# A fused forward and backward kernel on one core: plain loads in place of transposing and scattered ones at the start, and another order of the first transposes

## The chip, the cores and the metric

The kernel runs on one core of a Trainium2 chip. The metric is the device time of one execution in microseconds; the time before is the median of three runs. A second source is the profile of one further execution, with a record of every instruction on every engine and of every transfer. All positions in time below ("at 21.0 us") are counted from the start of that profiled execution.

## What is computed

The reference runs a block forward and then differentiates it with respect to all inputs but `B_x`; the kernel writes the output and eight gradients.

```python
mod = (silu(c) @ w_mod).reshape(1, 6, 1, -1)        # c: 1 x 576, w_mod: 576 x 3456
sa, ca, ga, sb, cb, gb = (mod[:, i] for i in range(6))
h = layernorm(x) * (1 + ca) + sa                    # x: 1 x 2048 x 576, bf16
x = x + ga * irfft2(rfft2(h) * (w_r + 1j * w_i))
h = layernorm(x) * (1 + cb) + sb
x = x + gb * (((h @ w_gate) * (h @ w_up)) @ w_down) # w_down: 4608 x 576
# outputs: x, and the vector-Jacobian product for grad_out (2048 x 576)
```

Three things of this matter for the change. The gate `gb` is one of the six modulation rows, so it needs `silu(c)` and a sixth of `w_mod`. The gradient that flows back into the hidden layer is `(gb * grad_out) @ w_down^T`; it needs `grad_out` turned so that the model dimension lies on the partitions, scaled by `gb`, and `w_down` turned likewise. And `x` is normalised and modulated before the Fourier transform.

## The kernel before

All of SBUF is one tile, `arena`, cut by byte offsets into views; PSUM is one tile, `bank`, of eight banks. Work is written out by hand for TensorE (PE): its instructions run in the order of the program. The order of VectorE (DVE), ScalarE (ACT), GpSimd (POOL) and SyncE (SP) is set by a scheduler, and each of them then runs its list strictly in that order. SP issues nearly all loads, POOL issues the stores of `ghh_d`.

The start of the kernel (lines 207 to 245) issues the first loads on SP in this order: `c` spread over 96 partitions (L209), a sixth of `w_mod` called `wm_a` (L212), `grad_out` in four groups `go` (L217), the first two of eighteen blocks of `w_down` by a transposing DMA (`load_wdT`, L232 and L233, two DMAs a block), `x` in four groups `xs` (L237), two more pieces of `w_mod` (`wm_b`, `wm_c`, L212 again), and the Fourier tables `TB`, `TC`, `TI`, `TBI` (L241 to L245). ACT issues `BD`, which holds the identity for transposes (L215). POOL issues four further small loads of `c` in other column layouts (L222 to L224).

PE then computes `gb` as a column (L257: 30 matmuls of one column each), turns `grad_out` into `goT` (`go_transposes`, L301: 80 transposes; ACT at L304 and DVE at L306 copy each group of four out of PSUM, 512 wide, times the `gb` column), and comes to the normalisation.

A queue called `fill` holds PE work that may go anywhere: 18 blocks of `w_down` by two couples, each couple four pieces (L324, L328, L331, L332), each block giving 256 rows of the hidden gradient; ACT copies them out (L336) and POOL stores them (L337). Block p needs its turned `w_down` block; the piece that starts block p asks for block p + 2 (`f0`, L340). `fill.run(us)` takes pieces off the queue until their nominal cost reaches the credit given. So the credits, not the clock, decide how much of this work lies between other stages.

Then, for each of four groups `jg` of `x`: `norm1(jg + 1)` (row statistics on DVE at L367 and L368, an inverse square root by small DVE operations L374 to L381, and the rows on ACT at L553), modulation and folding on DVE (L567, L568, L387, L388), `fill.run(7.5)`, the first Fourier stage `stage_a` on PE (L394, L397, L398) with its copy on ACT (L404, L412), and one pair of modulation rows (`mod_rows`, L272, copied out at L275 by ACT and L277 or L279 by DVE). PSUM banks 0 to 2 go round between the transposes, `stage_a` and `mod_rows` through `single()`.

Later stages: eight units of the middle Fourier stages, then a loop of 17 steps for the inverse transform and the second layer norm (L524 to L538 on PE, L532, L533, L685 to L687, L703, L704 on DVE, 2.7 us of `fill` each step), a flush of what is left in `fill`, and the block over the hidden layer (L745 to L756), whose right-hand side `h2T` comes by four transposing DMAs (`ln2_turn`, L690). From there on nothing is touched by the change.

Of the kernel before, what the change touches and what calls it, by code (L numbers as in the profile page):

```python
# [81 lines left out]
def build(ctx, tc, A_x, A_w_r, A_w_i, B_w_gate, B_w_up, B_w_down, c_in, w_mod, grad_out,  # L82
# [52 lines left out]
    def span(base, n, size):  # L135
        return [base + i * size for i in range(n)]
# [61 lines left out]
    wm_a, wm_b, wm_c = V(ST, [6, D]), V(ST + 71168, [6, 2 * D]), V(ST + 6912, [6, 3 * D])  # L198
    wm_t = {SGB: wm_a, SSA: wm_b[:, :, 0:D], SCA: wm_b[:, :, D:], SGA: wm_c[:, :, 0:D], SSB: wm_c[:, :, D:2 * D], SCB: wm_c[:, :, 2 * D:]}
    sc_rep = V(ST + 27648, [6, 128])  # L200
    h1_r = Ring([ACC + 24832, ACC + 29440], [4, D])
    st_r = Ring([ACC + 24224, ACC + 24416], [4, 2, 6], FP32)
    mv_r = Ring([ACC + 24608, ACC + 24640], [4, 2], FP32)
# [1 line left out]

    with tc.manual_schedule(engines={PE}):

        with nc.allow_non_contiguous_dma(reason="tiny c load"):
            sp.dma_start(c_bf[0:96, :], c_in[0, :].rearrange("(m q) -> q m", q=96))  # L209

        def load_wm(eng, t, s0, s1):
            eng.dma_start(t[0:96], w_mod[:, s0 * D:s1 * D].rearrange("(m q) n -> q m n", q=96))  # L212

        load_wm(sp, wm_a, 5, 6)
        ac.dma_start(BD.rearrange("p a b -> p (a b)"), tabs["BD"][:, :])  # L215
        for jg in range(4):
            sp.dma_start(go[:, 4 * jg:4 * jg + 4, :], go_v[:, 4 * jg:4 * jg + 4, :])  # L217
        ve.memset(ones[:], 1.0)
        po.memset(c2_bf[:], 0.0)
        with nc.allow_non_contiguous_dma(reason="tiny c loads"):  # L220
            for h in range(2):
                po.dma_start(c2_bf[64 * h:64 * h + 64, 0:9], c_in[0, :].rearrange("(m q) -> q m", q=64))  # L222
            po.dma_start(c2_bf[:, 9:13], c_in[0, 0:512].rearrange("(m q) -> q m", q=128))
            po.dma_start(c2_bf[0:64, 13:14], c_in[0, 512:576].rearrange("(m q) -> q m", q=64))  # L224

        wdt = {}

        def load_wdT(p):
            t = WdT_r.next()
            wdt[p] = t  # L230
            rows = B_w_down[256 * p:256 * p + 256, :]
            sp.dma_start_transpose(out=t[:, 0:4, :], in_=rows[:, 0:512])  # L232
            sp.dma_start_transpose(out=t[:, 4, :], in_=rows[:, 448:576])  # L233

        load_wdT(0)
        for jg in range(4):
            sp.dma_start(xs[:, 4 * jg:4 * jg + 4, :], x_v[:, 4 * jg:4 * jg + 4, :])  # L237
            if jg == 0:
                load_wm(sp, wm_b, 0, 2)
        load_wdT(1)  # L240
        sp.dma_start(TB.rearrange("p a b -> p (a b)"), tabs["TB"][:, :])  # L241
        load_wm(sp, wm_c, 2, 5)
        sp.dma_start(TC.rearrange("p a b c -> p (a b c)"), tabs["TC"][:, :])
        sp.dma_start(TI.rearrange("p a b c -> p (a b c)"), tabs["TI"][:, :])
        sp.dma_start(TBI.rearrange("p a b -> p (a b)"), tabs["TBI"][:, :])  # L245


        q96 = slice(0, 96)
        ve.tensor_copy(c_f[q96], c_bf[q96])
        act(sig[q96], c_f[q96], ACT.Sigmoid)  # L250
        tt(sc_bf[q96], c_f[q96], sig[q96], MUL)
        for m in range(6):
            ve.tensor_copy(sc_rep[q96, m, :], sc_bf[q96, m:m + 1].to_broadcast([96, 128]))
        for dk in range(5):
            d0 = 448 if dk == 4 else 128 * dk
            for m in range(6):
                mm(bank[:, 0, dk:dk + 1], wm_a[0:96, m, d0:d0 + 128], sc_bf[0:96, m:m + 1], m == 0, m == 5)  # L257
        ve.tensor_copy(gb_bf[:], bank[:, 0, 0:5])
        ve.tensor_copy(gbcol[:], gb_bf[:])

        sbank = [0]

        def single():
            sbank[0] = (sbank[0] + 1) % 3
            return sbank[0]
# [14 lines left out]

        def silu_columns():

            c2, s2 = small[:, 82:96], small[:, 50:64]
            c2_bf_all = c2_bf[:, :]
            ve.tensor_copy(c2, c2_bf_all)
            act(s2, c2, ACT.Sigmoid)
            tt(c2_bf_all, c2, s2, MUL)
            ve.tensor_copy(sc64, c2_bf[:, 0:9])
            t = dsl5
            ts(t, s2[:, 9:14], -1.0, 1.0, MUL, ADD)  # L290
            tt(t, t, c2[:, 9:14], MUL)
            ts(t, t, 1.0, None, ADD)
            tt(t, t, s2[:, 9:14], MUL)

        def go_transposes(jg):
            for m in range(5):
                b = single()
                pt = bank[:, b, 0:256].bitcast(BF)
                d0 = 448 if m == 4 else 128 * m
                for jj in range(4):  # L300
                    pe.transpose(pt[:, 128 * jj:128 * jj + 128], go[:, 4 * jg + jj, d0:d0 + 128], ident)  # L301
                dst = goT[:, m, 512 * jg:512 * jg + 512]
                if m % 2 == 0 or jg == 0:
                    act(dst, pt, ACT.Copy, scale=gbcol[:, m:m + 1])  # L304
                else:
                    ts(dst, pt, gbcol[:, m:m + 1], None, MUL)  # L306


        dpair = [0]
# [7 lines left out]
        def ghh_couple(p, sb):  # L317

            b0 = [0, 0]
            cs = [slice(512 * (sb + i), 512 * (sb + i) + 512) for i in range(2)]  # L320

            def full_a(i):
                for k, m in enumerate(range(4)):
                    mm(bank[:, b0[i], :], wdt[p][:, m, 0:128], goT[:, m, cs[i]], i == 0 and k == 0, i == 1 and k == 3)  # L324

            def full_b(i):
                for k, m in enumerate((0, 1, 2, 4)):
                    mm(bank[:, b0[i] + 1, :], wdt[p][:, m, 128:256], goT[:, m, cs[i]], i == 0 and k == 0, i == 1 and k == 3)  # L328

            def rem(i):  # L330
                mm(bank[:, b0[i], :], wdt[p][64:128, 4, 0:128], goT[64:128, 4, cs[i]], i == 1, i == 0)  # L331
                mm(bank[:, b0[i] + 1, :], wdt[p][0:64, 3, 128:256], goT[0:64, 3, cs[i]], i == 1, i == 0)  # L332

            def evac(i):
                st = ghst_r.next()
                ac.copy(st[:], bank[:, b0[i]:b0[i] + 2, :])  # L336
                po.dma_start(ghh_d[p, :, :, cs[i]], st[:])  # L337

            def f0():
                if sb == 0 and p + 2 < NP:  # L340
                    load_wdT(p + 2)
                b0[0] = dbank()
                b0[1] = dbank()
                full_a(0)

            def f1():
                full_b(0)
                rem(0)
                evac(0)
                rem(1)  # L350

            def f3():
                full_b(1)
                evac(1)
            fill.add(0.87, f0)
            fill.add(1.4, f1)
            fill.add(0.87, lambda: full_a(1))
            fill.add(0.87, f3)

        for p in range(NP):  # L360
            for sb in (0, 2):
                ghh_couple(p, sb)


        def row_stats(src, st, mv, jj):
# [42 lines left out]
        def evac_rem(eng, brem, j0, n):  # L408
            dst = At[0:64, 4, :, 8 * j0:8 * (j0 + n)].rearrange("p c (j b) -> p j c b", j=n)
            src = bank[0:64, brem, 0:128 * n].rearrange("p (j c b) -> p j c b", j=n, c=16)  # L410
            if eng is ac:
                ac.copy(dst, src)  # L412
            else:
                ve.tensor_copy(dst, src)
# [130 lines left out]
        def norm1(jg):  # L545
            j0 = 4 * jg
            st, mv = st_r.next(), mv_r.next()
            for jj in range(4):
                row_stats(xs[:, j0 + jj, :], st, mv, jj)
            inv_std(mv, rstd1, nmr1, j0)  # L550
            h1s[jg] = h1_r.next()
            for j in range(j0, j0 + 4):
                act(h1s[jg][:, j - j0, :], xs[:, j, :], ACT.Identity, bias=nmr1[:, j:j + 1], scale=rstd1[:, j:j + 1])  # L553

        norm1(0)
        for jg in range(4):
            go_transposes(jg)
        silu_columns()
        fill.run(7.0)
        mod_rows(SSA)  # L560
        mod_rows(SCA)
        for jg in range(4):
            j0 = 4 * jg
            if jg < 3:
                norm1(jg + 1)
            h1 = h1s[jg]
            tt(h1[:], h1[:], opca_b, MUL)  # L567
            tt(h1[:], h1[:], sa_b, ADD)  # L568
            fold(Ft[:, j0:j0 + 4, :], h1, 4)
            fill.run(7.5)  # L570
            for jj in range(4):
                b = single()
                stage_a(Ft[:, j0 + jj, :], b)
                evac_a(ac, b, j0 + jj)
            for jj in range(4):
                stage_a_rem(Ft[:, j0 + jj, :], 3, jj)
            evac_rem(ac, 3, j0, 4)
            mod_rows((SGA, SSB, SCB, SGB)[jg])


# [827 lines left out]
```

## Time and profile before

| | |
|---|---|
| Median of 3 runs | 1545.58 us (1545.24 to 1550.46) |
| Profiled execution: device time | 1546.08 us |
| Profiled execution: first to last instruction | 1544.3 us |
| Mean granted PE clock | 0.987 |
| PE busy | 1474.5 us, 95% |
| DVE busy | 782.4 us, 51% |
| ACT busy | 556.2 us, 36% |

A line of a profile page's part with engines gives busy time and share of the span. In a window table each line is one stretch of time: the busy time of each engine with the number of its instructions in brackets, then the granted PE clock (1.00 is full speed), the mean busy share of the 16 DMA engines, and the rate of all transfers in GB/s. In a table of waits a line reads "who (engine, tile, line) <- who released it: total us, how often, longest". In a timeline a line has a start, a duration, the engine, the line of the program and the operation.

### The profile page before, as it was taken

Reading aid. Unit: us, or ns where it says so; the run is one execution under the profiler, and the core shown is the slowest. Engines: PE = TensorE matmul, PEld = TensorE weight load, DVE = VectorE, ACT = ScalarE, POOL = GpSimd, SP = SyncE. Lnnn points to the kernel's source line nnn. Section 1 sums busy time; section 2 is a strip of 40 time slices with the busy share of each in tenths; the row PEclk is TensorE's granted clock in tenths of the full one; section 3 lists DMA queues with packets and bytes.
Section 4 is the critical chain, followed back from the end, with each engine's and each line's share of the span. In section 5 each row is a group of like instructions: output and inputs, shape, how many; then the busy total and the mean of one; then the engine's idle time right before and its main releaser. Section 6 shows DMA issues by size and latency. Waiting matters only on the chain.

```text
span 1544.3 us, 28343 instructions
## 1 busy us (share of the span) xinstructions
PE 1474.5 (95%) x11213; PEld 984.0 (64%) x11236; DVE 782.4 (51%) x1733; ACT 556.2 (36%) x1064; POOL 265.3 (17%) x389
## 2 busy tenths in 40 slices
PE   6799998999999999999999999999999988899997
PEld 3344443586686677677667668668667676676665
DVE  5523487533533533543543453353354775787555
ACT  5656676212203212212221221220321575334664
POOL 1122422122122112112202202211201101000000
PEclk9899999999999999999999999999999999999998
DMA  9765787885476467558548557657645679797752
GB/s 251 211 142 162 200 234 182 182 176 134 110 153 157 114 131 167 123 112 183 124 96 183 130 111 157 142 113 144 162 114 106 157 192 295 194 245 198 200 171 86
DMA packets 444903, 248.77 MB, mean 161 GB/s; under 512 B 323104, under 2 KB 422240, under 8 KB 444256
## 3 DMA queue, kind: packets, MB, share of 16 engines
q1 hardware_dynamic: 421376, 176.53, 51.2%
q0 software_dynamic: 22624, 69.62, 15.1%
q8 instruction: 88, 1.44, 0.4%
q10 hardware_dynamic: 768, 0.79, 0.2%
q14 instruction: 47, 0.39, 0.1%
HBM read 95.58 MB, written 74.20 MB: 110 GB/s over the span
## 4 chain that ended last, share of the span: by engine, by line
PE 72%; issue 16%; DVE 4%; DMA 3%; SPq 3%; ACT 2%; POOL 0%; POOLq 0%; DVEq 0%; ACTq 0%
PE bank L750 8%; PE bank L781 8%; PE bank L752 8%; PE bank L828 7%; PE bank L832 7%; PE bank L887 5%; PE bank L889 4%; PE bank L890 4%; PE bank L888 4%; PE bank L324 3%; PE bank L328 3%; PE bank L745 2%; PE bank L848 2%; DMA arena<-in_B_w_down_dram 1%; SPq L232 1%
## 5 line engine op out<-in xcount | busy, mean ns | idle before, releaser
L901 DVE TENSOR_TENSOR arena<-arena,bank 128x576 f32<-128x576 f32 x256 | 193.0, 754 | 305.2 <-PE bank L890 305.2
L756 ACT CAST arena<-bank 128x512 bf16<-128x512 f32 x144 | 84.4, 586 | 391.0 <-PE bank L746 373.6
L887 PE MATMUL bank<-arena 128*128 128x288 bf16 x576 | 164.3, 285 | 3.0 <-ACT arena L833 2.8
L890 PE MATMUL bank<-arena 128*128 128x288 bf16 x576 | 164.9, 286 | 0.0
L889 PE MATMUL bank<-arena 128*128 128x288 bf16 x576 | 164.7, 286 | 0.0
L888 PE MATMUL bank<-arena 128*128 128x288 bf16 x576 | 164.4, 285 | 0.0
L750 PE MATMUL bank<-arena 128*128 128x512 bf16 x576 | 149.4, 382 | 1.0 <-ACT arena L756 1.0
L828 PE MATMUL bank<-arena 128*128 128x256 bf16 x1152 | 149.7, 273 | 0.6 <-ACT arena L833 0.6
L1025 PE MATMUL bank<-arena 128*128 128x288 bf16 x1152 | 149.7, 287 | 0.0
L832 PE MATMUL bank<-arena 128*128 128x256 bf16 x1152 | 149.3, 273 | 0.0
L752 PE MATMUL bank<-arena 128*128 128x512 bf16 x576 | 148.7, 381 | 0.0
L1025 PEld LDWEIGHTS <-arena 128*128 128x128 bf16 x1152 | 111.8, 98 | 31.7 <-issue 3.3
L781 PE MATMUL bank<-arena 128*128 128x288 bf16 x1024 | 128.1, 286 | 0.0
L828 PEld LDWEIGHTS <-arena 128*128 128x128 bf16 x1152 | 110.9, 98 | 17.6 <-issue 4.6
L832 PEld LDWEIGHTS <-arena 128*128 128x128 bf16 x1152 | 112.3, 98 | 13.7 <-issue 0.4
L833 ACT CAST arena<-bank 128x256 bf16<-128x256 f32 x144 | 53.5, 372 | 185.3 <-PE bank L832 185.3
L781 PEld LDWEIGHTS <-arena 128*128 128x128 bf16 x1024 | 100.2, 98 | 28.2
L760 DVE TENSOR_TENSOR arena<-arena 128x512 bf16<-128x512 bf16 x144 | 61.2, 425 | 107.4 <-ACT arena L756 107.4
L750 PEld LDWEIGHTS <-arena 128*128 128x128 bf16 x576 | 50.4, 98 | 79.8 <-issue 31.8
L752 PEld LDWEIGHTS <-arena 128*128 128x128 bf16 x576 | 56.6, 98 | 68.6 <-issue 1.1
L757 ACT CAST arena<-bank 128x512 bf16<-128x512 f32 x144 | 84.8, 589 | 23.7 <-PE bank L752 23.7
L336 ACT CAST arena<-bank 128x1024 bf16<-128x1024 f32 x72 | 72.7, 1010 | 53.3 <-PE bank L332 25.8
(247 smaller groups left out, 2243.1 us busy)
## 6 DMA issues: line engine op xcount, KB each, us to landing
ghh_d<-arena POOLq DMA_DIRECT2D x72, 256.0 KB, 3.5
arena<-ghh_d POOLq DMA_DIRECT2D x36, 512.0 KB, 5.4
hh_d<-arena SPq DMA_DIRECT2D x36, 512.0 KB, 4.3
arena<-hh_d SPq DMA_DIRECT2D x16, 1152.0 KB, 7.2
out_dram<-arena POOLq DMA_DIRECT2D x36, 256.0 KB, 5.1
arena<-in_B_w_down_dram POOLq DMA_DIRECT2D x18, 288.0 KB, 4.1
out_dram<-arena POOLq DMA_DIRECT2D x36, 144.0 KB, 5.5
arena<-in_B_w_gate_dram POOLq DMA_DIRECT2D x18, 256.0 KB, 3.5
```

The lines of the kernel that those rows point to most:

```text
L750: mm(bank[:, bg, :], w[:, m, fs], h2T[:, js, m, :], odd == 0 and m == 0, odd == 1 and m == 3)
L752: mm(bank[:, bu, :], w[:, 4 + k, fs], h2T[:, js, m, :], odd == 0 and k == 0, odd == 1 and k == 3)
L757: ac.copy(u[:], bank[:, bu, :])
L781: mm(bank[:, b0 + h, 0:288], sf[:, 0, fb, j, :], go[:, j, 288 * h:288 * h + 288], j == 0, j == 15)
L828: mm(bank[:, st["b"], 0:256], h2p[:, j, 128 * m:128 * m + 128], sf[:, 1 + w, :, j, :], j == 0, False)
L832: mm(bank[:, st["b"], 0:256], h2p[:, j, 128 * m:128 * m + 128], sf[:, 1 + w, :, j, :], False, j == 15)
L887: mm(o, xT[:, 1, 0, cs], wT[p][:, 0, 0, hs], True, False)
L888: mm(o, xT[:, 2, 0, cs], wT[p][:, 0, 1, hs], False, False)
L889: mm(o, xT[:, 1, 1, cs], wT[p][:, 1, 0, hs], False, False)
L890: mm(o, xT[:, 2, 1, cs], wT[p][:, 1, 1, hs], False, True)
L901: tt(dst, dst, src, ADD)
L1025: mm(bank[:, yb, 0:288], hl[:, fb % 18, 128 * (j % 2):128 * (j % 2) + 128], wdr[:, fb, 288 * h:288 * h + 288], fb == 0, fb == 35)
```

## The change

The change touches only the first part of the program.

1. `c` comes as one row on one partition (`c_row`, 1,152 B). 29 matmuls of one column against a one spread it into the column layouts that were loaded before; POOL's four loads and its memset are gone.
2. Blocks 0 to 2 of `w_down` come as plain loads (`wdn`, rows of 1,152 B) into the area that `At` takes later. `turn_wd` turns each with ten PE transposes into two banks, and ACT copies them out (1024 and 256 wide). Block 0 is turned among the gradient's transposes; blocks 1 and 2 are pieces of `fill`, with a nominal cost of 1.2 us each, after the first couple of blocks 0 and 1. Blocks from 3 on come by the transposing DMA as before.
3. The order of the loads on SP is new; `go` 0 is first after `c_row`.
4. The first 20 gradient transposes stand ahead of the gate on PE. Pairs of groups share a bank, and they are copied out 1024 wide, ten copies in place of twenty.
5. The rows of `norm1` are split off (`norm1_rows`) and written after `mod_rows` or after `stage_a`, not before.

```diff
-        with nc.allow_non_contiguous_dma(reason="tiny c load"):
-            sp.dma_start(c_bf[0:96, :], c_in[0, :].rearrange("(m q) -> q m", q=96))
...
-        load_wm(sp, wm_a, 5, 6)
+        sp.dma_start(c_row[0:1, :], c_in[0:1, :])
         ac.dma_start(BD.rearrange("p a b -> p (a b)"), tabs["BD"][:, :])
...
+        def load_wdn(p):
+            sp.dma_start(wdn[p][:], B_w_down[256 * p:256 * p + 256, :].rearrange("(j f) d -> f j d", f=128))
+
+        load_go(0)
+        load_wm(wm_a, 5, 6)
+        load_go(1)
+        load_wdn(0)
+        load_go(2)
+        load_go(3)
+        load_xs(0)
+        load_wm(wm_b, 0, 2)
+        load_wdn(1)
+        load_xs(1)
+        load_xs(2)
+        load_wdn(2)
+        load_xs(3)
+        sp.dma_start(TB.rearrange("p a b -> p (a b)"), tabs["TB"][:, :])
+        load_wm(wm_c, 2, 5)
...
-        po.memset(c2_bf[:], 0.0)
-        with nc.allow_non_contiguous_dma(reason="tiny c loads"):
-            for h in range(2):
-                po.dma_start(c2_bf[64 * h:64 * h + 64, 0:9], c_in[0, :].rearrange("(m q) -> q m", q=64))
-            po.dma_start(c2_bf[:, 9:13], c_in[0, 0:512].rearrange("(m q) -> q m", q=128))
-            po.dma_start(c2_bf[0:64, 13:14], c_in[0, 512:576].rearrange("(m q) -> q m", q=64))
...
-        load_wdT(0)
-        for jg in range(4):
-            sp.dma_start(xs[:, 4 * jg:4 * jg + 4, :], x_v[:, 4 * jg:4 * jg + 4, :])
-            if jg == 0:
-                load_wm(sp, wm_b, 0, 2)
-        load_wdT(1)
...
+        def turn_wd(p, b0, b1):
+
+            t = wdt[p] = WdT_r.t[p % 3]
+            for b, m0, m1 in ((b0, 0, 4), (b1, 4, 5)):
+                pt = bank[:, b, :].bitcast(BF)
+                for m in range(m0, m1):
+                    d0 = 448 if m == 4 else 128 * m
+                    for fb in range(2):
+                        c0 = 256 * (m - m0) + 128 * fb
+                        pe.transpose(pt[:, c0:c0 + 128], wdn[p][:, fb, d0:d0 + 128], ident)
+                ac.copy(t[:, m0:m1, :].rearrange("p m f -> p (m f)"), pt[:, 0:256 * (m1 - m0)])
...
-        ve.tensor_copy(c_f[q96], c_bf[q96])
+        cp = bank[:, 5, 128:160]
+        for m in range(6):
+            mm(cp[0:96, m:m + 1], c_row[0:1, 96 * m:96 * m + 96], ones[0:1, 0:1], True, True)
+        ve.tensor_copy(c_f[q96], cp[q96, 0:6])
...
+        GB = ((0, 1, 2, 3, 4), (5, 0, 1, 2, 3))
+        for m in range(5):
+            turn_go(0, m)
         for dk in range(5):
             d0 = 448 if dk == 4 else 128 * dk
             for m in range(6):
-                mm(bank[:, 0, dk:dk + 1], wm_a[0:96, m, d0:d0 + 128], sc_bf[0:96, m:m + 1], m == 0, m == 5)
+                mm(bank[:, 5, dk:dk + 1], wm_a[0:96, m, d0:d0 + 128], sc_bf[0:96, m:m + 1], m == 0, m == 5)
...
+        for m in range(5):
+            turn_go(1, m)
+            evac_go(0, m)
+        turn_wd(0, 6, 7)
+        for jg in (2, 3):
+            for m in range(5):
+                turn_go(jg, m)
+                if jg == 3:
+                    evac_go(1, m)
...
-                if sb == 0 and p + 2 < NP:
+                if sb == 0 and 3 <= p + 2 < NP:
                     load_wdT(p + 2)
...
         for p in range(NP):
             for sb in (0, 2):
                 ghh_couple(p, sb)
+                if sb == 0 and p < 2:
+                    fill.add(1.2, lambda p=p: turn_wd(p + 1, single(), single()))
...
+        silu_columns()
         norm1(0)
-        for jg in range(4):
-            go_transposes(jg)
-        silu_columns()
         fill.run(7.0)
         mod_rows(SSA)
         mod_rows(SCA)
+        norm1_rows(0)
...
             evac_rem(ac, 3, j0, 4)
+            if jg < 3:
+                norm1_rows(jg + 1)
             mod_rows((SGA, SSB, SCB, SGB)[jg])
```

## The prediction, made before the changed kernel was run

> **What bounds the kernel now.** I read the page's slices first: PE is busy nearly all the time, except at the very start, in the second slice and once near 265 us. Only there can a change of the first loads win or lose.
>
> ```profile
> PE   6799998999999999999999999999999988899997
> PEclk9899999999999999999999999999999999999998
> ```
>
> Then the windows of the first 60 us, the waits up to 62 us, and the timeline of the same stretch.
>
> ```profile
> 0.00:10.00 10.00, 0.96 (x30) 0.88 (x30) 1.53 (x9) 1.49 (x2) 3.32 (x9) 1.00 0.75 149
> 20.00:30.00 10.00, 9.75 (x62) 4.79 (x61) 9.00 (x36) 6.13 (x9) 1.39 (x2) 1.00 1.11 256
> 40.00:50.00 10.00, 6.26 (x43) 3.65 (x43) 9.19 (x37) 8.97 (x14) 0.69 (x1) 0.83 1.01 400
> 50.00:60.00 10.00, 6.02 (x20) 1.97 (x21) 5.78 (x16) 4.54 (x7) 1.23 (x2) 0.66 0.84 166
> ...
> PE bank L257 <- DMA arena<-in_w_mod_dram: 7.6, 1, 7.6
> PE bank L324 <- DMA arena<-in_B_w_down_dram: 4.7, 1, 4.7
> PE bank L394 <- ACT arena L404: 2.9, 1, 2.9
> PE bank L272 <- ACT arena L275: 1.4, 1, 1.4
> ```
>
> PE does 1 us of work in the first ten. The transfer engines are mostly full from 4 us to 58 us, yet move only 149 to 400 GB/s. Where PE waits at 40 to 58 us the granted clock falls to about half, so the matmuls after the wait cost double. The longest wait is for block 2 of `w_down`: its transposing loads occupy SP and land at 53.9 us.
>
> ```profile
> 4.18 6.66 SPq L232
> 15.84 9.61 SPq L232
> ...
> 31.31 22.62 DMA arena<-in_B_w_down_dram
> 53.94 0.04 issue
> 53.98 1.89 PE bank L324 x4
> ```
>
> Last, the windows around the end of the first phase. In the 17-step loop DVE is the full engine (9.42 and 9.70 of 10), and after it PE idles, because SP has ten `w_gate`/`w_up` transposes ahead of the last `ln2_turn` (L690).
>
> ```profile
> 230.00:240.00 10.00, 9.95 (x56) 4.41 (x56) 9.42 (x37) 6.93 (x11) 2.60 (x5) 1.00 0.93 260
> 260.00:270.00 10.00, 4.81 (x24) 1.68 (x22) 3.95 (x11) 3.32 (x6) 0.00 (x0) 0.99 0.33 67
> ...
> 263.30 3.82 SPq L668 DMA_TRANSPOSE arena<-in_B_w_up_dram  x3
> 267.21 3.04 SPq L690 DMA_TRANSPOSE arena<-arena  x1
> ```
>
> **What the Trainium skill says.** "TensorE: Matmul & The Clock Gate", Part 1: the array runs at half clock when idle or cold, and at full clock after some 3.4 us of work. The trace agrees: four L328 take 1.71 us at clock 0.50 (from 55.87 us) and 0.86 us at 1.00 (from 67.07 us). Its Part 4 says that transposes don't raise the clock; here they go from 0.145 us apart (10.9 us) to 0.0885 us apart (18.4 us) with nothing else on PE between, so the measurement decides. "DMA: Bandwidth & Descriptors", Specifications, sets 512 B as the least size for full rate: in the first 5 us 608 of 1121 packets are smaller, and the mean is 115 GB/s. The same page's Anatomy gives about 2 us fixed per transfer (stated for POOL's path); `BD`, issued by ACT, took 2.7 us for 128 KB.
>
> **The start.** Removed: five scattered loads of `c` (SP 0.40 us to issue, POOL 1.67 + 0.80 + 0.56), landing 3.3 to 8.1 us after issue; POOL has nothing else to do until 24 us. Six transposing DMAs, which cost SP 6.66 + 1.66 + 9.61 + 2.06 + 3.23 + 15.94 = 39.2 us of its queue. Added on SP: three loads of 288 KB, some 0.5 us each like L217. SP's 18 issues now take about 9 us, so the transfers' rate and not the queue sets the landings. The trace shows 400 to 428 GB/s in 42 to 50 us and 256 in 20 to 30 us; I take 400, first bytes at 2.3 us and 0.7 us for the completion. Adding up KB in the new order: `go` 0 lands at 4.9 us, `wm_a` 6.5, `go` 1 8.0, `wdn` 0 8.7, `go` 3 11.6, `xs` 0 13.1, `wm_b` 16.5, `wdn` 1 17.3, `wm_c` 28 to 30. `c_row`, a single row, should land at 2.9 to 4 us. It is a new wait ahead of all of PE's queue, but `go` 0 ends later.
>
> PE: 29 matmuls of one column (30 L257 took 0.96 us) end by 4.7 us; 20 transposes at the cold 0.145 us, 4.9 to 7.8; gate, 7.8 to 8.9; `go` 1, to 11.3; block 0 of `w_down`, ten transposes, to 12.3; `go` 2 and 3 at 0.0885 us, held by copies, to 16.0. Copies: a 512-wide one costs 687 ns on ACT (L304) and 484 on DVE (L306). From L336 (1024 wide, 1010 ns) against L756 (512 wide, 586) 424 ns are added per 512 on ACT, so 1.11 us; I take 1.0 on DVE. Starting at 10.0 us, after the gate and the moved `silu_columns`, ACT does three, then the two of block 0 (1.01 + 0.30), to 14.7, then three more to 18.0, which only the second couple needs. So the fill starts at 16.0 us, not 21.00: **5.0 us** won, with block 0 turned in it.
>
> **Up to the second `stage_a`.** Norm 0 on DVE comes after four copies, 17.0 to 23.2 us (6.18 before, L367 at 21.24 to L381). Fill, 7.1 us: to 23.1. In ACT's new order two rows of `norm1` (L553 before) stand ahead of the copies of turned block 1, and behind those the copies of `mod_rows`. The rows wait for DVE until 23.2. Then 2 x 0.79, 1.3 (block 1), 0.8, 1.0, 0.8, so that the first `mod_rows` copy ends at 29.3. PE's four half rows (0.79 each) share three banks with block 1, and wait 1.9 + 2.0 us in place of 1.4 before. They end at 30.2 us (32.7 before). The next fill is 7.6 us, `stage_a` 2.4 without the wait of 2.92 (the rows now stand behind its copies), `mod_rows` 1.6 at full clock where it took 2.8: 41.8 us, against 48.4. The next fill, 7.3 us, has no wait for block 2, which PE has turned: saves 4.74, and about 2 us of half-clock matmuls. Second `stage_a` at **49.1 us** against 62.47.
>
> There ACT has three rows of group 2 ahead of the copies: about 2.3 us of wait against 0.6. After that stage and its `mod_rows`: 55.0 against 66.2, **11.2 us** won. Bounds of the ACT waits together: none (3.9 + 2.3 us more gain) to double (as much less).
>
> **What it adds elsewhere.** PE's 30 turns (30 x 0.0885 = 2.7 us) and ACT's six copies (3.9 us) are inside these sums. Their credit of 2.4 us pushes 2.4 us of couples to the flush at about 250 us. I cost that at nothing, because PE then idles for `h2T` (7.3 us at L745, from 262 us). Its bounds are 0 and 2.4. `load_wdT(3)` waits for block 0's last matmul as before, and lands behind the tables about 40 us, needed at 59. `At` overwrites `wdn`: the last turn stands before the first `stage_a` on PE, so no wait. From 66 to 200 us PE is busy 91 to 99%, so a shift passes on. In the loop DVE has the same work. In SP's new order nine, not ten, of the 1.24 us transposes stand ahead of the last `ln2_turn`: **1.2 us** more. Later orders are the same but for a few neighbours.
>
> Sum: 11.2 + 1.2 = 12.4 us on the profile's span of 1544.3. That run's device time was 1546.1, the median of the three 1545.6: 1545.6 - 12.4 = **1533.2 us**.
>
> **The rivals.**
> - ACT's order takes the place of the transfers: rows that wait for DVE hold the copies that PE needs. For: DVE is 8.9 to 9.2 of 10 in 20 to 50 us, and 2.92 us were lost so before. Against: ACT has only some 19 us of work in the 33 us from 16 to 49. Waits doubled: 12.4 - 6.2 = 6.2, **1539.4**.
> - Those waits don't come, as DVE finishes its rows early: 12.4 + 6.2, **1527.0**. Against: the DVE chain of 17 to 23 us is measured.
> - The first loads don't land earlier, since rows of 1,152 B run no faster than the 256 GB/s of 20 to 30 us: the fill starts at about 21 again and 5.0 are lost: **1538.2**. For: `wm_a` took 6.3 us for 648 KB before, though beside the scattered loads. That the change would do nothing of what it says falls here; the six transposing loads are gone in any case.
> - Slower: the 17-step loop. DVE is its bound, and the scheduler has put its DVE and SP lists in another order. If ACT's copies of displaced couples or the moved `ln2_turn` hold DVE, each row pays. It decides from 12.4 / 17 = 0.73 us a row; at 1 us a row 1545.6 - 12.4 + 17 = **1550.2**. Against: same operations, same credit a step.
>
> **How the numbers follow.** Chances: forecast 0.56 (1529.5 to 1537.5), ACT's order 0.14, no waits 0.12, slow first loads 0.10, loop 0.08. The range, 1526 to 1541, leaves out the loop's case and the far end of ACT's. What a measurement here can tell from no change is about 0.5%, 7.7 us, so faster means below 1537.9: 0.53 + 0.12 + 0.10 from the two cases near the border = 0.75; same 0.17; slower 0.08.
>
> **What would show it.** First L324 near 16 us, no wait of PE for `in_B_w_down` in the first 60 us, granted clock near 1.00 from 20 to 60 us, second `stage_a` near 49 us, waits of `mod_rows` on ACT of about 4 us, the wait at L745 shorter by 3 to 4 us. I am wrong if the fill starts after 19 us, if ACT holds PE for over 10 us in the first 60, or if the loop takes longer than from 200 to 251 us.

## The result, and the profile after

| | before | after |
|---|---|---|
| Median | 1546.0 us (4 runs) | 1532.95 us (4 runs, 1525.74 to 1533.61) |
| Ratio | | 0.9899 [0.9864, 0.9934] |
| Profiled execution, first to last instruction | 1544.3 us | 1531.7 us |
| PE busy | 1474.5 us | 1476.4 us |
| First matmul of the first couple | 21.0 us | 15.1 us |
| First `stage_a`, second `stage_a` | 40.8, 62.5 us | 37.6, 49.5 us |
| First matmul of Fourier stage B | 90.4 us | 77.7 us |
| 17-step loop, start | 181.7 us | 169.8 us |
| First matmul of `w_down`'s gradient | 311.1 us | 299.1 us |

The forecast was 1533.2 us, in a range of 1526 to 1541. Twice more the changed kernel was run on other chips as a reference: ratios of 0.9889 [0.9873, 0.9906] and 0.9892 [0.9877, 0.9907].

The page's slices, after:

```profile
PE   7999998999999999999999999999999989899997
PEclk9999999999999999999999999999999999999998
```

Only the first two slices differ from before by a step or more that matters (6 and 7 tenths there). The windows of the first 60 us (stretch, its length, busy time of PE, PEld, DVE, ACT, POOL, then PE's clock, the transfers' busy share and GB/s):

```profile
0.00:10.00 10.00, 5.49 (x83) 5.07 (x84) 1.83 (x15) 1.71 (x3) 0.19 (x4) 1.00 0.84 255
20.00:30.00 10.00, 7.14 (x44) 4.25 (x45) 6.51 (x29) 6.04 (x10) 1.37 (x2) 0.83 1.05 365
40.00:50.00 10.00, 9.28 (x57) 4.51 (x59) 8.65 (x32) 9.62 (x15) 1.38 (x2) 1.00 1.12 315
50.00:60.00 10.00, 8.12 (x50) 4.05 (x49) 7.32 (x8) 8.19 (x13) 2.04 (x3) 0.83 0.34 100
```

PE has 5.5 us of work in the first ten (1.0 before) and 9.3 and 8.1 where it had 6.3 and 6.0. But 20 to 30 us is worse than before (7.1 against 9.8): a wait stands there that I had not forecast. The waits of PE up to 62 us, without those for the very first loads (2.4 us for `c`, 1.7 for `grad_out`) and two of 0.2 and 0.3 us:

```profile
PE bank L262 <- DMA arena<-in_B_w_down_dram: 3.7, 1, 3.7
PE bank L442 <- ACT arena L452: 1.7, 1, 1.7
PE bank L333 <- DMA arena<-in_w_mod_dram: 0.8, 1, 0.8
PE bank L442 <- ACT arena L263: 0.4, 1, 0.4
```

L262 is the turn of a `w_down` block, L333 `mod_rows`, L442 `stage_a`, L452 its copy, L263 the copy of a turned block. PE waits 3.7 us for block 1 in place of 4.7 us for block 2, and no longer for the copy of `mod_rows` (L336, L275 before). In the timeline the wait and what it costs afterwards:

```profile
22.86 1.25 PE L262 MATMUL bank<-arena 128*128 128x128 bf16 x10 [3.67 <-DMA arena<-in_B_w_down_dram]
23.90 1.91 PE L370 MATMUL bank<-arena 128*128 128x512 bf16 x4
...
49.48 0.83 PE L442 MATMUL bank<-arena 128*128 128x128 bf16 x12
51.97 0.38 PE L442 MATMUL bank<-arena 128*128 128x128 bf16 x4 [1.66 <-ACT arena L452]
```

The four L370 behind the wait take 1.91 us, not 1.04: half clock again. The second `stage_a` starts at 49.48 us.

SP runs late with plain loads as well: 5.5 us pass between the load of `wm_c` (L214) and that of `TC` (L240). The view of SP's own waits says what for, here and at two more loads (L220 is `x`): each time for the landing of an earlier load.

```profile
16.51 0.33 SPq L214 DMA_DIRECT2D arena<-in_w_mod_dram  x1
22.34 1.70 SPq L240 DMA_DIRECT2D arena<-tab_TC  x1
...
SPq L240 <- DMA arena<-in_w_mod_dram: 5.5, 1, 5.5
SPq L220 <- DMA arena<-in_w_mod_dram: 2.0, 1, 2.0
SPq L214 <- DMA arena<-in_A_x_dram: 1.4, 1, 1.4
```

Counted along SP's order, the tensor named is each time that of the load eight places ahead: `wm_b` for `TC`, `wm_a` for the second group of `x`, the first group of `x` for `wm_c`. So this program seems to keep at most eight loads of SP under way; that is an inference from the names. It fits e6 below, where one moved load puts `x` eight places ahead of `TC`, and the view names `x` there (2.6 us). The kernel before has no such wait in its first 62 us: there SP stood inside the issue of transposing loads instead.

At the end of the first phase, the window of the wait for `h2T`, SP's queue ahead of the last `ln2_turn` (L742), and PE's wait (L797):

```profile
250.00:260.00 10.00, 7.11 (x35) 2.53 (x33) 4.95 (x13) 4.39 (x8) 0.00 (x0) 1.00 0.47 92
...
252.53 2.53 SPq L720 DMA_TRANSPOSE arena<-in_B_w_up_dram  x2
255.16 3.05 SPq L742 DMA_TRANSPOSE arena<-arena  x1
...
260.67 0.39 PE L797 MATMUL bank<-arena 64*128 64x512 bf16 x1 [3.56 <-DMA arena<-arena]
```

The wait is 3.6 us (7.3 before). In part this is because PE arrives with more couples left to flush, the 2.4 us that the turns displaced. `ln2_turn` is issued 12.05 us earlier than before (255.16 against 267.21), and the loop had started 11.9 us earlier: the win of the first 60 us has passed through the rest unchanged.

### The profile page after: what moved, and what is told of

The parts are those of the page before. It is cut to its first block, busy times and chain, and to the rows that moved or that the text cites. A ratio compares the mean times of both kernels' runs of the same rounds, so it can differ in the third digit from the quotient of the medians.

```text
span 1531.7 us, 28445 instructions
## 1 busy us (share of the span) xinstructions
PE 1476.4 (96%) x11272; PEld 988.3 (65%) x11295; DVE 783.3 (51%) x1733; ACT 557.2 (36%) x1062; POOL 262.4 (17%) x384
## 4 chain that ended last, share of the span: by engine, by line
PE 74%; issue 17%; DMA 4%; DVE 3%; ACT 2%; SPq 0%; POOL 0%; POOLq 0%; ACTq 0%; DVEq 0%
PE bank L802 9%; PE bank L833 8%; PE bank L804 8%; PE bank L880 8%; PE bank L884 8%; PE bank L939 5%; PE bank L941 4%; PE bank L942 4%; PE bank L940 4%; PE bank L370 3%; PE bank L374 3%; PE bank L797 3%; PE bank L900 2%; DMA arena<-in_w_mod_dram 2%; DMA arena<-x_d 1%
```

## The experiments

One execution differs from the next by 3 us and more, and a good part of that arises in the last 250 us: the last stage alone (first to last L1025 of the kernel before, 215.6 us) takes 214.9 to 221.1 us in these profiles, though nothing in it is touched. So beside the ratio I give a mark in the profile that lies ahead of it: the first matmul of `w_down`'s gradient (311.1 us before). The changed kernel's three profiles put it at 299.1, 295.7 and 296.9 us; a difference within that is none. The last two columns add up PE's waits that end between 4 and 66 us, for transfers and for ACT (in us).

| run | ratio to before, interval | mark, us | transfers | ACT |
|---|---|---|---|---|
| before | 1 | 311.1 | 14.6 | 5.9 |
| changed | 0.9899 [0.9864, 0.9934] | 299.1 | 6.2 | 2.3 |
| changed, second chip | 0.9889 [0.9873, 0.9906] | 295.7 | 6.0 | 2.8 |
| changed, third chip | 0.9892 [0.9877, 0.9907] | 296.9 | 6.2 | 2.3 |
| e1 before, rows split | 0.9999 [0.9987, 1.0011] | 311.6 | 18.9 | 3.5 |
| e2 changed, transposing loads | 0.9915 [0.9894, 0.9936] | 303.1 | 7.3 | 2.4 |
| e3 changed, scattered `c` | 0.9877 [0.9858, 0.9896] | 297.1 | 11.0 | 3.9 |
| e4 changed, rows inline | 0.9909 [0.9888, 0.9929] | 301.5 | 5.1 | 5.6 |
| e6 changed, block 1 earlier | 0.9916 [0.9898, 0.9934] | 297.5 | 6.8 | 3.2 |
| e8 changed, credits of 6.7 | 0.9882 [0.9861, 0.9904] | 295.0 | 6.6 | 2.4 |
| e10 before, block 2 earlier | 0.9980 [0.9971, 0.9990] | 308.1 | 9.7 | 7.1 |
| e11 changed, order of need | 0.9888 [0.9872, 0.9903] | 294.7 | 2.6 | 3.9 |
| e13 changed, old order of loads | 0.9963 [0.9951, 0.9975] | 305.6 | 17.4 | 0.9 |
| e14 e11 and e8 together | 0.9862 [0.9845, 0.9880] | 292.5 | 3.8 | 1.9 |

My theory at first: the transposing loads fill the transfer engines and hold SP's queue, and PE waits for them. The rival: what counts is something else, the order of ACT, the scattered `c`, or the place of each load in the queue.

**e1: the split of the rows alone, in the kernel before.**

```diff
             inv_std(mv, rstd1, nmr1, j0)
+
+        def norm1_rows(jg):
+            j0 = 4 * jg
             h1s[jg] = h1_r.next()
...
             evac_rem(ac, 3, j0, 4)
+            if jg < 3:
+                norm1_rows(jg + 1)
```

> The kernel before with part 5 alone: the rows of norm 1 stand behind the copies of stage_a and behind mod_rows. Theory (the landing of block 2 of w_down at about 54 us sets where PE goes on, and whatever is won ahead of it is lost at that wait): within 1.5 us of the kernel before, 1544.5 to 1547.5 us, with the wait of 2.9 us at the first stage_a gone and the wait for in_B_w_down longer by about as much (7 to 8 us, not 4.7). Rival (the order of ScalarE is a cost of its own): 2.5 to 4 us faster, 1542 to 1543.5.

Measured: 1547.35 us, no change. PE's waits show where the gain went:

```profile
PE bank L324 <- DMA arena<-in_B_w_down_dram: 8.5, 1, 8.5
PE bank L394 <- ACT arena L404: 0.7, 1, 0.7
```

The wait for ACT at `stage_a` fell from 2.9 to 0.7 us, and the wait for block 2 grew from 4.7 to 8.5. A gain ahead of a late transfer was worth nothing here.

**e2: transposing loads for blocks 0 to 2, in the new places.**

```diff
-        load_wdn(0)
+        load_wdT(0)
...
-        turn_wd(0, 6, 7)
...
-                if sb == 0 and p < 2:
-                    fill.add(1.2, lambda p=p: turn_wd(p + 1, single(), single()))
```

The same for blocks 1 and 2.

> The changed kernel with part 2 undone: blocks 0 to 2 of w_down by transposing DMAs, issued where the plain loads stood; no turns on PE. Theory (the transposing loads fill the transfer engines and hold SP's queue, and PE waits for them): 8 to 15 us slower than the changed kernel, 1541 to 1548 us, with waits for in_B_w_down or for loads queued behind it of over 8 us in the first 60. Rival (they cost little, the gain is in the other parts, and 30 transposes less on PE are worth 2.7 us): 1529 to 1535 us.

Measured: 1534.53 us, a cost of 0.16 to 0.26% (2.5 to 4 us) against the three runs of the changed kernel, with the intervals overlapping. The mark is 4.0 us later than the latest of them. Here my theory fell: 8 to 15 us were not lost. PE never waits for `w_down`; it waits longer for `wm_c` behind it:

```profile
42.84 3.06 PE L332 MATMUL bank<-arena 96*128 96x288 bf16 x12 [5.04 <-DMA arena<-in_w_mod_dram]
```

So the transposing kind costs some transfer time, but it was not the main thing. Without turns that displace couples, fewer are left to flush, and PE waits 8.0 us for `h2T`. What e2 keeps of the change is the new order of all loads, with block 2 ahead of the tables. That made a second theory: **the place in SP's queue**.

**e10: the kernel before, with block 2's transposing load ahead of `TC`, `TI` and `TBI`.**

```diff
+        load_wdT(2)
         sp.dma_start(TC.rearrange("p a b c -> p (a b c)"), tabs["TC"][:, :])
...
-                if sb == 0 and p + 2 < NP:
+                if sb == 0 and 3 <= p + 2 < NP:
```

> The kernel before with one load moved: the transposing load of block 2 of w_down is issued ahead of TC, TI and TBI, not behind them. Theory (what cost PE 4.7 us and a cold clock was the place in SP's queue, not the kind of load): no wait for in_B_w_down over 1 us at 49 to 54 us, 4 to 7 us faster than before, 1539 to 1543 us, about half of the whole change's gain. Rival (the transposing loads themselves are the cost, wherever they stand): within 1.5 us of before, with the wait moved to the piece of w_mod that is now behind or kept.

Measured: 0.9980, 3.1 us faster (1.5 to 4.5), less than the 4 to 7 that I expected, though the interval reaches into that. The wait for `w_down` is gone, as the theory says. The wait for ACT at the first `stage_a` is the old one (2.92 us before), and half clock follows it:

```profile
44.68 0.59 PE L395 MATMUL bank<-arena 128*128 128x128 bf16 x4 [2.93 <-ACT arena L405]
49.02 1.49 PE L329 MATMUL bank<-arena 128*128 128x512 bf16 x3 [0.22 <-issue]
```

The wait for ACT at the second `stage_a` grew from 0.6 to 1.7 us, and the stretches at half clock up to 70 us add up to 10.2 us, as before. That fits a gain of 3.1 us for a wait of 4.7.

**e13: the changed kernel with all loads in the old places, but plain** (block 0 stands behind the gradient again).

```diff
-        load_go(0)
         load_wm(wm_a, 5, 6)
+        load_go(0)
...
         load_xs(3)
+        load_wdn(1)
         sp.dma_start(TB.rearrange("p a b -> p (a b)"), tabs["TB"][:, :])
...
         sp.dma_start(TBI.rearrange("p a b -> p (a b)"), tabs["TBI"][:, :])
+        load_wdn(2)
```

> The changed kernel with part 3 undone: plain loads of w_down's blocks and all others in the places of the kernel before (wm_a ahead of the gradient, block 1 behind x, block 2 behind the tables). Theory (the order of the loads carries most of the gain): waits for in_B_w_down of some 10 us at block 1, 5 to 10 us slower than the changed kernel beside it. Rival (the kind of loads carries it, since plain ones leave the transfers free): less than 3 us slower.

Measured: 1541.33 us, 0.9963 against 0.9892 of the changed kernel on the same chip: 11 us lost of the 16.7 us that the change is worth there, slightly more than I expected. The intervals are apart. The timeline has both waits:

```profile
27.29 1.25 PE L262 MATMUL bank<-arena 128*128 128x128 bf16 x10 [7.25 <-DMA arena<-in_B_w_down_dram]
47.55 1.25 PE L262 MATMUL bank<-arena 128*128 128x128 bf16 x10 [6.81 <-DMA arena<-in_B_w_down_dram]
```

With plain loads, the order thus carries about two thirds of the gain. A part of this lies in the demand of the turns themselves. A block's turn stands in `fill` one couple ahead of its first use, so PE asks for block 1 at 20.0 us here; the kernel before used it first at 33.5 us and did not wait for it. No run moved the turns back in `fill`.

**e3: `c` by the scattered loads again.**

```diff
-        sp.dma_start(c_row[0:1, :], c_in[0:1, :])
+        with nc.allow_non_contiguous_dma(reason="tiny c load"):
+            sp.dma_start(c_bf[0:96, :], c_in[0, :].rearrange("(m q) -> q m", q=96))
...
+            po.dma_start(c2_bf[:, 9:13], c_in[0, 0:512].rearrange("(m q) -> q m", q=128))
```

> The changed kernel with part 1 undone: c comes by the five scattered loads of before (one on SP, four on GpSimd), without the 29 matmuls. Theory (the small elements hold the transfer engines for the first 4 us or so, so all first loads shift, but part of the shift disappears in the wait for block 1): first gradient transpose at 7.5 to 9 us, not 5.8; 1 to 3 us slower than the changed kernel, 1534 to 1536 us. Rival A (the scattered loads are what held the start back): 5 us slower or more, 1538 us up. Rival B (nothing): within 1 us of 1533.

Measured: 1528.99 us, 0.9877, not slower than the changed kernel's 0.9889 to 0.9899; the mark, 297.1, is within its spread. The start is late, as expected, but that costs nothing:

```profile
7.91 2.31 PE L285 MATMUL bank<-arena 128*128 128x128 bf16 x20 [7.91 <-DMA arena<-in_grad_out_dram]
...
24.83 0.73 PE L269 MATMUL bank<-arena 128*128 128x128 bf16 x10 [1.60 <-DMA arena<-in_B_w_down_dram]
```

The first couple starts at 19.0 us, 3.9 later than in the changed kernel. The wait for block 1 is 1.6 us, against 3.7, 2.5 and 2.8 in the changed kernel's three profiles, and the clock is 1.00 in all windows to 60 us, where each of the three has at least one at 0.83. Spreading `c` from one row is worth nothing that I can measure; rival B comes nearest, though the median is 4 us below its 1533.

**e4: rows of the norm inline again.**

```diff
             inv_std(mv, rstd1, nmr1, j0)
+            norm1_rows(jg)
...
-        norm1_rows(0)
...
-            if jg < 3:
-                norm1_rows(jg + 1)
```

> The changed kernel with part 5 undone: rows of norm 1 written right after the statistics again. Theory (no late load hides it now): the wait at the first stage_a comes back, 2 to 4 us slower than the changed kernel, 1535 to 1537 us. Rival (ScalarE's order is set by the scheduler and by VectorE's pace in either case): within 1 us of 1533.

Measured: 1533.93 us; 0.9909 lies 0.10 to 0.20% above the changed kernel, within the intervals. The profile is clearer than the time: the mark is 2.4 us behind the latest of the changed kernel's three, and the wait at the first `stage_a` is back.

```profile
40.40 0.87 PE L442 MATMUL bank<-arena 128*128 128x128 bf16 x8 [2.90 <-ACT arena L263]
```

By the ratio it is 1.5 to 3.1 us slower, which touches the theory's 2 to 4. But the median is within 1 us of 1533, as the rival said, so the time alone does not settle it.

**e6: block 1's load behind the gradient, ahead of `x` and `wm_b`** (one line moved).

```diff
         load_go(3)
+        load_wdn(1)
         load_xs(0)
         load_wm(wm_b, 0, 2)
-        load_wdn(1)
```

> The changed kernel with the plain load of block 1 issued right behind the gradient, ahead of x and of w_mod. Theory (the wait of 3.7 us at 19 to 23 us and the half clock after it are a loss of some 5 us, of which 2 to 4 come back as waits of mod_rows for ScalarE): 1 to 3 us faster than the changed kernel beside it. Rival (the transfers are full in any case, and wm_b and wm_c land later by as much): within 1 us, with PE's wait moved to in_w_mod.

Measured: 1534.83 us, against 1530.10 beside it; not faster, and the intervals overlap. The rival's mechanism was right: PE gets past block 1 and waits for `wm_c`, with which it can start at 41.3 us, not at 39.8 to 40.7.

```profile
41.32 3.06 PE L333 MATMUL bank<-arena 96*128 96x288 bf16 x12 [4.55 <-DMA arena<-in_w_mod_dram]
```

**The changed kernel again**, as reference for e6, e8 and e10, and once more for e11 and e13:

> The changed kernel once more, on the same chip as the three beside it, as their reference; 1530 to 1535 us. Theory for the spread (the granted clock drops in some executions in the last 250 us, where PE often waits): the first matmul of the gradient of w_down in the steady part (the line with sf and go, at 299.1 us in the changed kernel) repeats within 2 us, and what spreads comes after it.

> The changed kernel as reference for the two beside it: 1529 to 1534 us; first of its 1024 steady matmuls of w_down's gradient at 295 to 299 us.

Measured: 1530.10 and 1529.46 us. The marks are 295.7 and 296.9, so with the first profile they repeat within 3.4 us, not 2; the wait for `h2T` was 3.6, 0.4 and 1.4 us in the three. A part of the spread thus arises before the tail.

**e8: fewer couples in the groups.**

```diff
-            fill.run(7.5)
+            fill.run(6.7)
```

> The changed kernel with credits of 6.7 in place of 7.5 in the four groups: 3.2 us of couples move from the groups to the flush ahead of the hidden-layer block. Theory (PE idles there for h2T for 3.6 us, so couples cost nothing there; this is why the 2.4 us that the turns displaced cost nothing): 2 to 3.5 us faster than the changed kernel beside it, that wait down to under 1 us. Rival (VectorE's and ScalarE's pace bounds the groups, so PE only waits more there): within 1 us.

Measured: 1529.10 us against 1530.10: within the noise. PE's wait for `h2T` is gone, but it was only 0.4 us in the reference beside it. Inconclusive on its own.

**e11: loads in the order of need.**

```diff
         load_xs(0)
-        load_wm(wm_b, 0, 2)
         load_wdn(1)
+        load_wm(wm_b, 0, 2)
         load_xs(1)
         load_xs(2)
         load_wdn(2)
+        load_wm(wm_t[SGA], 2, 3)
         load_xs(3)
+        load_wm(wm_t[SSB], 3, 4)
+        load_wm(wm_t[SCB], 4, 5)
         sp.dma_start(TB.rearrange("p a b -> p (a b)"), tabs["TB"][:, :])
-        load_wm(wm_c, 2, 5)
```

> The changed kernel with its loads in the order in which PE needs them: block 1 ahead of wm_b, and wm_c cut in three, its first third (for SGA) ahead of x 3, the rest and TB behind it. Theory (the start is bound by transfers: all that is needed for the first mod_rows of SGA lands at 40 to 41 us wherever PE stands, and a wait costs half clock on top): no wait of PE for in_B_w_down or in_w_mod over 1 us between 10 and 62 us, granted clock at 1.00 from 20 to 50 us, 2 to 5 us faster than the changed kernel beside it. Rival (ScalarE's and VectorE's chain of norms binds just behind the transfers): waits for ScalarE take their place and the time is within 1.5 us.

Measured: 1529.48 against 1529.46 us: the rival. No transfer makes PE wait over 0.5 us between 10 and 62 us, and the first `stage_a` starts at 33.8 us, 2.0 earlier than beside it. Then ACT's copies make it wait:

```profile
41.84 1.02 PE L372 MATMUL bank<-arena 128*128 128x512 bf16 x4 [0.97 <-ACT arena L384]
49.02 0.58 PE L444 MATMUL bank<-arena 128*128 128x128 bf16 x4 [2.26 <-ACT arena L454]
```

The mark is 2.2 us earlier; the time does not show it.

**e14: e11 and e8 together.**

> Both at once: loads in the order of need, and credits of 6.7 in the four groups. Theory (no transfer waits are left before 62 us, and couples in the flush stand in PE's wait for h2T, which is 1.5 us with the first edit alone): the second Fourier stage starts near 71.5 us (74.6 with the first edit alone), the wait for h2T falls under 0.5 us, and the first matmul of w_down's gradient comes 1 to 2 us earlier than its 294.7 us; ratio to the kernel before 0.986 to 0.989. Rival (groups shortened on PE run into VectorE's chain of norms): no earlier, with more waits for ScalarE and VectorE at stage_a.

Measured: 1526.15 us, 0.9862 [0.9845, 0.9880], the fastest median of all, and the mark at 292.5 is 3.2 us ahead of the changed kernel's best. Its interval overlaps that of the changed kernel (0.9889 and 0.9892), so it is faster than before, but that it is faster than the change is not shown by the time. The expected mechanism holds in part: the wait for `h2T` is gone and the mark came 2.2 us earlier, but a wait of 1.6 us for `w_mod` at 24 us is left, and stage B starts at 74.5 us as in e11, not at 71.5. In the groups PE meets DVE's folding, as the rival said:

```profile
45.86 0.28 PE L444 MATMUL bank<-arena 128*128 128x128 bf16 x2 [0.74 <-DVE arena L437]
48.20 0.58 PE L444 MATMUL bank<-arena 128*128 128x128 bf16 x4 [0.94 <-ACT arena L454]
```

Not tried: the first 20 transposes and the paired copies (part 4) alone. In e3 a first couple 3.9 us later made no difference, so I expect none, but that is an argument and no measurement. Nor was the turn of block 1 tried later in `fill`: in the changed kernel PE asks for it at 19.2 us, the load lands at 22.8, and the first couple of block 1 starts at 32.1. There may be room to hide that wait.

## Why the prediction was right, and where by luck

The total, 12.4 us, met 13.05 in the medians and 12.6 in the spans. Point by point:

- **The start, 5.0 us.** The first couple moved from 21.0 to 15.1 us, 5.9. But the step was no gain of its own. e3 takes 3.9 us of it away and loses nothing, because PE only waits less for block 1 afterwards. The sum would have been wrong if I had priced part 1 alone.
- **The landings.** This is the step that failed. I took 400 GB/s and no delay by SP. Block 1 was used at 22.86 us, not 17.3, and `wm_c` at 40.66, not 28 to 30. So there was a wait of 3.67 us plus half clock where the prediction said none, and one of 0.82 us for `wm_c`. The rate was the main error: 255, 298, 365 and 283 GB/s in the four windows of the first 40 us. `wm_b` and `wm_c` moved at 222 to 227 (last section); at that rate their 3.3 MB take some 6.5 us longer than at 400, an estimate, of the 11 to 13 that `wm_c` was late. SP's issues ended at 25.1 us, not after about 9.
- **ACT's waits at `mod_rows`, 3.9 us.** They did not come: `mod_rows` ran in one piece from 27.41 to 30.53 us. I put this down to block 1, which held PE so long that DVE and ACT were done when it arrived. That is argued, not shown: in e6 and e11 block 1 is on time and the waits are 0.9 us and none, but there ACT has the copies of turned block 1 ahead of the rows, not behind them. The two errors cancelled, 3.9 forecast for ACT against 3.7 found for the transfer; that was luck. That is how 41.8 us for the next fill became 42.4, and 49.1 us for the second `stage_a` became 49.48. The two other profiles have it at 50.8 and 50.2 us.
- **The second `stage_a`'s wait, 2.3 us:** 1.66. After its `mod_rows`: 55.0 forecast, 55.05 found, 11.2 us won.
- **Block 2, 4.74 us and the clock.** The wait went, but not because PE turns the block. e2 shows that a transposing load in the new place does it too, e10 that moving this one load in the old kernel does, and e13 that a plain load in the old place loses about 11 us. The prediction had credited the kind of load, and the change had moved it as well. Nor did the 39.2 us of SP's queue go with the kind of load alone: in the new order of e2 the same six issues took 19.4 us, and with plain loads SP waits too, for earlier loads to land.
- **The displaced couples at nothing:** the wait for `h2T` fell from 7.3 to 3.6 us and work behind it kept the 12 us, which agrees, as do the 8.0 us of e2. e8 was meant to show it and could not.
- **SP's order, 1.2 us:** not found. Nine transposes took as long as ten had (242.5 to 255.1 us against 254.3 to 267.1), and the gain at `ln2_turn` is 12.05 against 11.9 at the loop's start.
- **The rivals.** ACT's order did not replace the transfers, nor did the loop slow down. The case of late first loads came true in that loads were late (block 1, `wm_c`), but neither in its place, the start of the fill, nor in its cause: `w_down`'s rows of 1,152 B ran at the pace of `x`, and the rows of `w_mod` were slow at every length.
- **Two readings.** The transposes before start 0.107 us apart at 10.9 us and 0.055 us apart at 18.4 us. My 0.145 and 0.0885 are the lengths of whole stretches divided by their counts, with gaps and the end of the last one in them. That the pace doubles stands. And the longest wait in the lines is the one of 7.6 us for the first piece of `w_mod`; that for block 2 is the longest after the start.

What the gain consists of, by the runs: the order of the loads some 11 us, given plain loads and turns where they stand (e13); the kind of load some 2.5 to 4, given the new order (e2, intervals overlapping); the rows on ACT about 1.5 to 3 by the ratio, within the noise, and 2.4 to 5.8 by the mark, once no late load hides it (e4, and e1 for the opposite); one-row `c` nothing (e3). Put the other way round, the new order without plain loads keeps some 13 of the 16 to 17 us, plain loads without the new order some 6. These don't add up to the total, since each wait hides the others.

## What to carry to other kernels

At a start that is bound by transfers, list each load with the time at which it is first needed and issue in that order; a load asked for by the loop that uses it stands behind everything that was issued up front. This has an end: in e11 the last step in that direction removed PE's waits for transfers and moved them to ACT, and the time stayed. Count, too, how long before its first use you ask for a load. Price a part only at the next wait downstream: whatever ends before a late transfer is absorbed there, so undo parts singly before you say which one paid. And when a forecast meets the total, look whether its terms were met.

## What the runs showed of the hardware

Sizes and durations of single packets in the trace's transfer records, first 60 us of the changed kernel, give bytes per ns of one of the 16 transfer engines:

```
row of                     bytes   packets   mean ns   bytes per ns
grad_out, x                 4608      1024     197.6           23.3
w_down, blocks 0 and 2      1152       512      51.1           22.6
w_down, block 1             1152       256      75.8           15.2
wm_a                        1152       576      73.4           15.7
wm_b                        2304       576     162.0           14.2
wm_c                        3456       576     229.7           15.0
```

Block 1 moved while `wm_b` was still on its way, blocks 0 and 2 beside `grad_out` and `x`. The windows show the same: no `w_mod` in the first, almost only `wm_b` in the second, almost only `wm_c` in the third.

```profile
8.00:13.00 5.00, 4.45 (x68) 4.25 (x67) 2.62 (x12) 2.94 (x4) 0.00 (x0) 1.00 1.03 406
14.00:20.00 6.00, 5.14 (x39) 2.44 (x37) 4.83 (x15) 5.27 (x7) 0.84 (x1) 1.00 1.04 227
28.00:34.00 6.00, 5.94 (x38) 3.42 (x39) 4.84 (x15) 2.81 (x5) 1.09 (x2) 1.00 1.03 222
```

So the rows of `w_mod` move at some 60 to 70% of the pace of `x`, and their length is not the reason: rows of 1,152 B of `w_down` keep up with `x`. In the kernel before, `wm_b` and `wm_c` ran at 13.9 and 17.3 bytes per ns. This is the main reason why my 400 GB/s were too much. Why those rows are slow is open; they go to 96 partitions where the others go to 128, and lie 6,912 B apart in memory, and no run varied either. 512 B as the least size for full rate (the Trainium skill, "DMA: Bandwidth & Descriptors", Specifications) does not explain it, since all of these rows are longer.

In the kernel before, the packets of 256 B that the transposing loads of blocks 0 and 1 bring took 24.1 ns each in block 0 and 51.1 in block 1, 10.6 and 5.0 bytes per ns.

The clock turns a wait into more than itself. After 3.67 us of waiting four L370 took 1.91 us, not 1.04; after one of 1.66 us, at 52 us, the matmuls at 55 us ran at half clock too, while after the same wait of 1.66 us in its second profile none did. The length of a single wait does not decide it: 2.5 and 2.8 us for block 1 in the second and third profile left the clock at 1.00, and the waits there of 1.8 us for `wm_c` were followed by half clock. Where the clock fell in the first 300 us of these profiles, it stayed at half for 3.41 us or two or three times as long. A part of the gain of each removed wait can be this.
